# ScalarE copies ahead of the gate product, shorter score folds and fixed tree buffers in a two-layer transformer kernel

## The chip, the core and the metric

The kernel runs on one core of a Trainium2 chip. The metric is the device time of one execution in microseconds (us), as the median of several executions. A profile shows one further look at the kernel: one execution, recorded by the hardware profiler, whose times are counted from the first instruction ("the span"). The engines are called PE (TensorE, matrix products; PEld is its weight load), DVE (VectorE), ACT (ScalarE), POOL (GpSimd) and SP (SyncE, here the queue that issues nearly all DMAs).

## The reference

Two layers, each an attention block (A) and a gated feed-forward block (B), on x of 2048 tokens by 1024 features in bf16:

```python
x = x + A(layernorm(x), wqkv, wo)
x = x + B(layernorm(x), w1, w3, w2)      # twice, with the same weights

# A: 32 heads of 32; a token sees itself and 7 tokens before it, 2 apart
logits[h, s, w] = sum_d q[h, s, d] * k[h, s - 2*w, d] * scale     # w = 0..7
o[h, s, :] = sum_w softmax(logits)[h, s, w] * v[h, s - 2*w, :]
# B: F = 3584
out = (silu(x @ w1) * (x @ w3)) @ w2
```

So the attention has no large matrix product: each score is a sum over 32 products of a query and a shifted key, and each output a sum over 8 weighted values.

## The kernel before

**Units and stages.** The tokens are cut into chunks of 512 (`CH`), so each layer has four units (l, c). The feed-forward block of a unit is `b_stage`. After the first layer's q, k and v (`first_q`, `q_part`, to about 197 us in the profile), units 0 and 1 run plain products with w1, w3 and w2 and at the same time prepare the weights for what follows: sums of squares on ScalarE (`measure`, L854), a matmul with ones that adds them over the partitions (`scales`, L868, "size"), scaled copies on ScalarE (`copies`, L881), differences of blocks on VectorE (`differences`, L892) and stores of the blocks to DRAM on POOL's queue (L894, L895, tile `t_d`). This is called the preparing stage below (197 to 526 us). From unit 2 on (about 574 us to the end) `products` uses the stored blocks: each 2 by 2 block product is made of seven products P1 to P7 in place of eight (a Strassen scheme in Winograd's form).

**Product stage.** One group is 256 columns of hidden features of w1 (m = 0, the gate) or w3 (m = 1, the up product), two tiles of 128, over the four blocks of features and tokens. Each of the seven products is eight matmuls of 256 columns (`run`, L1102), into PSUM banks called A, B and D (tile `st`). `head_part` (L1120 to L1161) writes down the order: P1, P5, P6 and P2 of one group ("early") alternate with P7, P3 and P4 of the group before ("late"). Between them stand: ScalarE's copies of bank A to B after P1 (L1128), of D to the snapshot `s5` after P5 (L1133) and of A to `su` after P6 (L1137); VectorE's D += su (L1140), which P3 waits for, and s22 = A + s5 after P7 (L1150). Snapshots lie in the tile `big`. `consume` (L1106) takes the four results q = 0 (P2), 3 (P7), 1 (P3) and 2 (P4). For the gate group it is a Silu with a per-partition scale on ScalarE (L1111, tile `sg`), for the up group one `scalar_tensor_tensor` on VectorE (L1116): result times scale times gate, written as 16-bit floats into `hT` (`h16` is the same memory). The second product of the block, with w2, is `W` (L1028; matmuls L1037), fed by sums of `hT` blocks on VectorE (L1008).

**Attention.** It is done in halves of 256 tokens (`TCH`), sixteen in all, mostly on VectorE and beside TensorE's products of other units. `score_steps` multiplies q by a shifted k for each of eight offsets (L581: 128 partitions x 8 x 256, bf16) and folds the eight rows of each product to one by three additions (`tree`: 4 and 2 rows at L505, 1 row at L507) into `psm`. `gather_heads` (L594) adds the partitions of each head by four matmuls with 32 columns of weights, one to each quarter of the partitions of the PSUM tile `L`. The softmax follows on VectorE (L614, L617, L623, L625, L626) with the exponential on ScalarE (L618). `spread_heads` (L635) brings the weights back to all partitions by four matmuls, which ScalarE copies to `At` (L637). `value_steps` does the same with v (L665, the same `tree`) into `oT`, and `o_tile` (L770) multiplies by wo and adds to x (L775). The buffers of the products are the pool `scr`, four tiles of 4 KB a partition; a tree writes its folds in place.

**What sets the order.** The order of instructions on PE, DVE, ACT and SP is the order in which the Python code emits them, by hand. A small planner keeps clocks (`now`) with assumed costs. VectorE's background steps (norms, `makes` = the block differences, `adds`, values, scores) are generators, and `background(until)` (L136) places steps that end by that time ahead of the next foreground instruction. ScalarE's background (norm passes `act_norm`, L313 and L340; sums of squares of w2, L932) is placed by `act_background` (L356) when it ends within 2.2 us after TensorE's planned time. Gathers and spreads wait in `pe_queue` until 1.5 us past the planned end of their input (L559). `between` and `o_tile` place the wo products. The costs are constants in the code, such as 1.14 for a product, 0.605, 0.34 and 0.205 for the folds, and 0.69 for the up group's multiply. So an edit to a cost, or to the number of steps, moves all later background work on every queue.

Of the kernel before, what the change touches and what calls it, by code (L numbers as in the profile page):

```python
# [8 lines left out]
BF16 = mybir.dt.bfloat16  # L9
FP16 = mybir.dt.float16  # L10
I32 = mybir.dt.int32
ALU = mybir.AluOpType
# [5 lines left out]
def kernel(  # L18
# [52 lines left out]
    xtp = ctx.enter_context(tc.tile_pool(name="xnT", bufs=2))  # L71
    scr = ctx.enter_context(tc.tile_pool(name="scr", bufs=4))
    wk = ctx.enter_context(tc.tile_pool(name="wk", bufs=1))
# [23 lines left out]
    def dve(cost, ready=0.0):  # L97
        now["dve"] = max(now["dve"], ready) + cost
        return now["dve"]
# [85 lines left out]
    hT = const.tile([P, HTN, CH], BF16, name="hT")  # L185
    zero = wk.tile([P, W, TCH], BF16, name="psm")
    nc.vector.memset(zero[:, 0:2, :], 0.0)
# [11 lines left out]
    snaps = [big[:, 3072 + 1024 * i:4096 + 1024 * i].bitcast(FP32) for i in range(4)]  # L199
    snaps = [s_.rearrange("p (a t) -> p a t", a=2) for s_ in snaps]  # L200
    blocks = [big[:, 3584 * i:3584 * (i + 1)].rearrange("p (b k c) -> p b k c", b=7, k=KT // 2) for i in range(2)]
    NG = NF // FG
# [291 lines left out]

    def tree(n, mul, dst):

        bufs = {}

        def first(i):
            bufs[i] = mul(i)  # L500

        def half(i, m):
            b = bufs[i]
            if m > 1:
                nc.vector.tensor_tensor(b[:, 0:m, :], b[:, 0:m, :], b[:, m:2 * m, :], op=ALU.add)  # L505
            else:
                nc.vector.tensor_tensor(dst(i), b[:, 0, :], b[:, 1, :], op=ALU.add)  # L507

        def product(i):
            return 1.14, 0.0, lambda: first(i)  # L510

        def fold(i, m):
            return {4: 0.605, 2: 0.34, 1: 0.205}[m], 0.0, lambda: half(i, m)


        yield product(0)
        yield fold(0, 4)
        for i in range(0, n, 2):
            yield product(i + 1)
# [46 lines left out]
    def score_steps():  # L566

        V = nc.vector
        for g, (l, h) in enumerate(halves):
# [5 lines left out]
            qT, kT, ready = qks[l, h]  # L575
            psm = wk.tile([P, W, TCH], BF16, name="psm")

            def mul_qk(w_):
                pr = scr.tile([P, KT, TCH], BF16, name="pr", tag="scr")
                k0 = HALO - DIL * w_  # L580
                V.tensor_tensor(pr[:], qT[:], kT[:, :, k0:k0 + TCH], op=ALU.mult)  # L581
                return pr
# [8 lines left out]
            def gather_heads(t):  # L591
                at["L"] = L = side.tile([P, W, BLK], FP32, name="L", tag="sd")
                for a in range(4):
                    nc.tensor.matmul(L[32 * a:32 * (a + 1), :, :], lhsT=gather[:],  # L594
                                     rhs=psm[:, :, a * BLK:(a + 1) * BLK], start=True, stop=True)
                at["t"] = pe(3, t) + 0.2
# [49 lines left out]
    def value_steps():  # L646

        V = nc.vector
        for g, (l, h) in enumerate(halves):
# [10 lines left out]

            def mul_v(t):
                tm = scr.tile([P, W, TCH], BF16, name="tm", tag="scr")
                base = vT[:, t, HALO:HALO + TCH]
                win = bass.AP(vT.tensor, base.offset, [list(base.ap[0]), [-DIL, W], [1, TCH]])
                V.tensor_tensor(tm[:], At[:], win, op=ALU.mult)  # L665
                return tm
# [322 lines left out]
    def products(u, f0, f1, hold):  # L989
# [116 lines left out]
        def consume(G, q, src, r):  # L1106
            m, g, f = G["m"], G["g"], G["f"] + 2 * (q % 2)
            inv = down_scale[:, m, g:g + 1]
            if m == 0:
                sg = gates[g, q] = sgp.tile([P, 2, HT], BF16, name="sg", tag="sg")  # L1110
                nc.scalar.activation(sg[:], src, ACTF.Silu, scale=inv)  # L1111
                G["t", q] = act(0.6, r, "silu")
            else:
                background(r + 0.8)
                t0 = HT * (q // 2)
                nc.vector.scalar_tensor_tensor(h16[:, f:f + 2, t0:t0 + HT], src, inv, gates[g, q][:],  # L1116
                                               op0=ALU.mult, op1=ALU.mult)
                dve(0.69, r)

        def head_part(i, name):  # L1120
# [220 lines left out]
```

## Time and profile before

| | us |
|---|---|
| median of 4 executions | 1562.84 (1560.77 to 1565.59) |
| the profiled execution, own time | 1561.34 |
| its span, first to last instruction | 1559.6 |
| PE busy | 1536.5 |
| DVE busy | 1256.8 |
| ACT busy | 842.2 |
| POOL busy | 114.1 |
| granted PE clock, mean share | 0.997 |

By stage (us from the span's start):

| stage | length | PE busy | DVE busy | ACT busy |
|---|---|---|---|---|
| start, 0 to 31 | 31 | 28.68 | 17.05 | 14.15 |
| first q, k, v, 31 to 197 | 166 | 163.02 | 132.16 | 111.53 |
| preparing stage, 197 to 526 | 329 | 322.69 | 272.69 | 215.56 |
| q, k, v, 526 to 574 | 48 | 46.87 | 40.78 | 17.18 |
| product stage with later q, k, v, 574 to 1556 | 982 | 975.24 | 793.55 | 483.79 |

How such lines are read: a row of a group gives the source line, the engine, the operation, output and input tiles with their shapes, the number of instructions, then busy time in us and the mean in ns of one, then the idle time of the engine just before them and what ended it ("<-"). A row of the timeline gives start and length in us, and in brackets the idle time before with what ended it. A row of waits gives who waited for whom, the sum in us, how often, and the longest. Matmuls are pipelined: one of 512 columns is shown as 0.379 us long while the next starts after 0.216.

### The profile page before, as it was taken

The numbers are of one execution on the slowest core, as the hardware profiler recorded it, in microseconds if no ns is written. First come the engines' busy times: TensorE is split into PE (matmuls) and PEld (weight loads), VectorE is DVE, ScalarE is ACT, GpSimd is POOL, SyncE is SP. The second block draws the span as 40 slices with busy tenths as digits, with TensorE's granted clock in tenths as the row PEclk, the third lists the DMA queues.
The fourth block names the chain that finished last, engine by engine and source line by source line (L and its number), as shares of the span: only waits on it lengthen the run. The fifth ranks groups of instructions, "written<-read, shape, count | busy, mean of one in ns | idle before, by whom it ended". The sixth has DMA issues, their size and how long they took to land.

```text
span 1559.6 us, 24976 instructions
## 1 busy us (share of the span) xinstructions
PE 1536.5 (99%) x9666; PEld 995.6 (64%) x9666; DVE 1256.8 (81%) x2186; ACT 842.2 (54%) x1319; POOL 114.1 (7%) x227
## 2 busy tenths in 40 slices
PE   9999999999899999999999999999999999999999
PEld 7666544444444568575685766867667667686865
DVE  4788898978968889998989996999698997646545
ACT  4785567666738345546373555554647336353432
POOL 0110001111111000001000030000200001000000
PEclk9999999999999999999999999999999999999999
DMA  9766869797888888988789887797979887888885
GB/s 333 195 205 190 230 176 350 259 290 274 254 280 269 289 279 299 311 297 259 266 298 309 290 260 247 265 347 280 311 257 307 298 293 258 311 277 339 308 297 203
DMA packets 258359, 431.16 MB, mean 276 GB/s; under 512 B 72832, under 2 KB 200064, under 8 KB 241984
## 3 DMA queue, kind: packets, MB, share of 16 engines
q1 hardware_dynamic: 248464, 390.90, 75.9%
q0 software_dynamic: 9632, 38.54, 6.4%
q8 instruction: 75, 1.23, 0.3%
q14 instruction: 44, 0.36, 0.1%
q10 hardware_dynamic: 144, 0.13, 0.0%
HBM read 345.90 MB, written 67.90 MB: 265 GB/s over the span
## 4 chain that ended last, share of the span: by engine, by line
PE 60%; DVE 2%; DMA 2%; ACT 1%; POOL 1%; issue 1%; ACTq 0%; DVEq 0%
PE st L1102 32%; PE w L1037 15%; PE ps L828 8%; PE po L770 5%; DMA wqkv<-in_A_wqkv_dram 1%; DMA t_d<-big 1%; PE pe L635 1%; POOL acc L317 1%; DVE tm L665 0%; DMA xnT<-xn 0%; ACT big L965 0%; DVE hT L1008 0%; DVE tm L505 0%; ACT xn L313 0%; DVE big L288 0%
## 5 line engine op out<-in xcount | busy, mean ns | idle before, releaser
L828 PE MATMUL ps<-xnT,wqkv 128*128 128x512 f16 (+1 forms) x1472 | 323.2, 379 | 1.1 <-DMA wqkv<-in_A_wqkv_dram 1.1
L1102 PEld LDWEIGHTS <-early 128*128 128x128 f16 x2688 | 262.6, 98 | 40.7 <-issue 1.5
L828 PEld LDWEIGHTS <-wqkv 128*128 128x128 bf16 x1472 | 210.5, 144 | 109.5 <-issue 1.8
L1037 PE MATMUL w<-t,hT 128*128 128x512 f16 x1008 | 226.8, 379 | 1.1 <-ACT big L1057 1.0
L1102 PEld LDWEIGHTS <-late 128*128 128x128 f16 x2016 | 197.3, 98 | 30.2 <-issue 1.1
L581 DVE TENSOR_TENSOR pr<-qT,kT 128x2048 bf16<-128x2048 bf16 x128 | 155.9, 1218 | 26.7 <-DMA qT<-qkv_d 14.3
L1102 PE MATMUL st<-xnT,late 128*128 128x256 f16 x1344 | 174.2, 273 | 0.8 <-DVE big L1150 0.8
L1102 PE MATMUL st<-big,early 128*128 128x256 f16 x1344 | 172.7, 273 | 1.7 <-DVE big L288 1.2
L1037 PEld LDWEIGHTS <-hT 128*128 128x128 f16 x1008 | 98.1, 98 | 113.8 <-issue 2.7
L1102 PE MATMUL st<-xnT,early 128*128 128x256 f16 x1344 | 165.7, 273 | 0.0
L665 DVE TENSOR_TENSOR tm<-At,vT 128x2048 bf16<-128x2048 bf16 x128 | 155.9, 1218 | 10.7 <-ACT At L637 10.7
L505 DVE TENSOR_TENSOR pr<-pr 128x1024 bf16<-128x1024 bf16 (+1 forms) x256 | 137.8, 551 | 0.5
L505 DVE TENSOR_TENSOR tm<-tm 128x1024 bf16<-128x1024 bf16 (+1 forms) x256 | 137.2, 551 | 0.4
L770 PE MATMUL po<-wo,oT 128*128 128x512 bf16 x512 | 115.7, 379 | 0.4 <-DVE x_sb L775 0.4
L1128 ACT COPY st<-st 128x512 f32<-128x512 f32 x84 | 48.3, 575 | 124.2 <-PE st L1102 120.7
L1116 DVE SCALAR_TENSOR_TENSOR hT<-st,down_scale,sg 128x512 f16<-128x512 f32 x126 | 94.0, 746 | 20.5 <-PE st L1102 19.8
L1223 PE MATMUL pu<-xnT,w3t 128*128 128x512 f16 x448 | 107.5, 383 | 0.0
L1111 ACT ACTIVATE sg<-st,down_scale 128x512 bf16<-128x512 f32 x126 | 87.0, 691 | 36.1 <-PE st L1102 34.4
L1214 PE MATMUL pg<-xnT,w1t 128*128 128x512 f16 x448 | 106.4, 380 | 0.0
L1140 DVE TENSOR_TENSOR st<-st,big 128x512 f32<-128x512 f32 x84 | 58.5, 696 | 53.7 <-ACT big L1137 53.7
L832 ACT CAST hT<-ps 128x512 bf16<-128x512 f32 x96 | 55.2, 586 | 82.1 <-PE ps L828 81.1
L1243 PE MATMUL acc<-w2t,hT 128*128 128x512 bf16 x448 | 97.8, 379 | 0.0
(168 smaller groups left out, 1863.3 us busy)
## 6 DMA issues: line engine op xcount, KB each, us to landing
early<-t_d SPq DMA_DIRECT2D x84, 1024.0 KB, 5.8
late<-t_d SPq DMA_DIRECT2D x84, 768.0 KB, 6.3
t<-t_d SPq DMA_DIRECT2D x42, 1024.0 KB, 6.8
t<-t_d SPq DMA_DIRECT2D x42, 768.0 KB, 5.2
wqkv<-in_A_wqkv_dram SPq DMA_DIRECT2D x28, 1024.0 KB, 7.3
w1t<-in_B_w_dram SPq DMA_DIRECT2D x14, 1024.0 KB, 7.8
w3t<-in_B_w_dram SPq DMA_DIRECT2D x14, 1024.0 KB, 9.7
t_d<-big POOLq DMA_DIRECT2D x28, 512.0 KB, 6.1
```

What stands on the lines that cost most here:

```text
L505: nc.vector.tensor_tensor(b[:, 0:m, :], b[:, 0:m, :], b[:, m:2 * m, :], op=ALU.add)
L581: V.tensor_tensor(pr[:], qT[:], kT[:, :, k0:k0 + TCH], op=ALU.mult)
L665: V.tensor_tensor(tm[:], At[:], win, op=ALU.mult)
L770: nc.tensor.matmul(ps[:], lhsT=oT[:, t, j * P:(j + 1) * P], rhs=wo[:, t, hh * 512:(hh + 1) * 512], start=(t == 0), stop=(t == KT - 1))
L828: nc.tensor.matmul(ps[:], lhsT=ws[kk // KH][:, kk % KH, t::KT], rhs=xnT[:, kk, :], start=(kk == 0), stop=(kk == KT - 1))
L1037: nc.tensor.matmul(out[:], lhsT=lhs[:, k, j * P:(j + 1) * P], rhs=w[:, k, :], start=start and k == 0, stop=k == nq - 1, skip_group_check=True)
L1102: nc.tensor.matmul(out[:, a, :], lhsT=w[:, a, blk, k, :], rhs=rhs[:, k, :], start=start and a == 0 and k == 0, stop=k == KQ - 1, skip_grou ...
L1111: nc.scalar.activation(sg[:], src, ACTF.Silu, scale=inv)
L1116: nc.vector.scalar_tensor_tensor(h16[:, f:f + 2, t0:t0 + HT], src, inv, gates[g, q][:], op0=ALU.mult, op1=ALU.mult)
L1214: nc.tensor.matmul(pg[:], lhsT=w1t[:, kk, fi * P:(fi + 1) * P], rhs=xnT[:, kk, :], start=(kk == 0), stop=(kk == KT - 1))
L1223: nc.tensor.matmul(pu[:], lhsT=w3t[:, kk, fi * P:(fi + 1) * P], rhs=xnT[:, kk, :], start=(kk == 0), stop=(kk == KT - 1))
L1243: nc.tensor.matmul(acc[:], lhsT=hT[:, f, j * P:(j + 1) * P], rhs=tiles[hh][f // nq][:, f % nq, :], start=(f == 0), stop=(f == f1 - f0 - 1))
```

## The change

Three edits. First, in the up group, three of the four results (q = 0, 1, 2) are copied by ScalarE from PSUM to bf16 in SBUF, with the scale applied; the fourth (q = 3) gets its scale in s22 on VectorE, also as bf16. The multiply with the gate becomes a plain `tensor_tensor` of two SBUF tiles. Second, the score trees stop at two rows, `psm` is twice as large, and each half has eight gather matmuls, the second four adding to the first in PSUM. Third, the pool `scr` goes, and each of the two trees works in one fixed tile of 12 rows (6 KB a partition): even steps use rows 0 to 7 for the product, odd steps rows 4 to 11. The order of steps in the score tree changes with it. Planned costs change with the first edit (0.69 to 0.34 for the multiply, 0.5 for a copy).

```diff
-    scr = ctx.enter_context(tc.tile_pool(name="scr", bufs=4))
...
-    zero = wk.tile([P, W, TCH], BF16, name="psm")
+    tree_bufs = [const.tile([P, 12, TCH], BF16, name=f"tree{i}") for i in range(2)]
+    zero = tree_bufs[0]
...
+    tight = big[:, 6144:7168].bitcast(BF16).rearrange("p (i a t) -> p i a t", i=2, a=2)
...
-    def tree(n, mul, dst):
+    def tree(n, buf, mul, dst, partial):
         def first(i):
-            bufs[i] = mul(i)
+            mul(i, buf[:, 0:8, :] if i % 2 == 0 else buf[:, 4:12, :])
         def half(i, m):
-            b = bufs[i]
-            if m > 1:
-                nc.vector.tensor_tensor(b[:, 0:m, :], b[:, 0:m, :], b[:, m:2 * m, :], op=ALU.add)
+            b = buf[:, 0:4, :] if i % 2 == 0 else buf[:, 8:12, :]
+            if m == 4:
+                nc.vector.tensor_tensor(b, b, buf[:, 4:8, :], op=ALU.add)
+            elif m == 2 and not partial:
+                nc.vector.tensor_tensor(b[:, 0:2, :], b[:, 0:2, :], b[:, 2:4, :], op=ALU.add)
             else:
-                nc.vector.tensor_tensor(dst(i), b[:, 0, :], b[:, 1, :], op=ALU.add)
+                nc.vector.tensor_tensor(dst(i), b[:, 0:m, :], b[:, m:2 * m, :], op=ALU.add)
...
             yield product(i + 1)
             yield fold(i, 2)
             yield fold(i + 1, 4)
-            yield fold(i, 1)
+            if not partial:
+                yield fold(i, 1)
+            if partial and i + 2 < n:
+                yield product(i + 2)
             yield fold(i + 1, 2)
-            if i + 2 < n:
+            if not partial and i + 2 < n:
                 yield product(i + 2)
-            yield fold(i + 1, 1)
+            if not partial:
+                yield fold(i + 1, 1)
             if i + 2 < n:
                 yield fold(i + 2, 4)
...
-            psm = wk.tile([P, W, TCH], BF16, name="psm")
+            psm = wk.tile([P, W, 2, TCH], BF16, name="psm")
...
-            yield from tree(W, mul_qk, lambda w_: psm[:, w_, :])
+            yield from tree(W, tree_bufs[0], mul_qk, lambda w_: psm[:, w_], True)
...
-                for a in range(4):
-                    nc.tensor.matmul(L[32 * a:32 * (a + 1), :, :], lhsT=gather[:],
-                                     rhs=psm[:, :, a * BLK:(a + 1) * BLK], start=True, stop=True)
+                for i in range(2):
+                    for a in range(4):
+                        nc.tensor.matmul(L[32 * a:32 * (a + 1), :, :], lhsT=gather[:],
+                                         rhs=psm[:, :, i, a * BLK:(a + 1) * BLK], start=i == 0, stop=i == 1,
+                                         skip_group_check=True)
...
-            yield from tree(KT, mul_v, lambda t: oT[:, t, :])
+            yield from tree(KT, tree_bufs[1], mul_v, lambda t: oT[:, t, :], False)
...
-                background(r + 0.8)
+                if q != 3:
+                    up = tight[:, 1] if q == 2 else sgp.tile([P, 2, HT], BF16, name="up", tag="up", bufs=1)[:]
+                    nc.scalar.activation(up, src, ACTF.Copy, scale=inv)
+                    src, r = up, act(0.5, r)
+                background(r + 0.5)
                 t0 = HT * (q // 2)
-                nc.vector.scalar_tensor_tensor(h16[:, f:f + 2, t0:t0 + HT], src, inv, gates[g, q][:],
-                                               op0=ALU.mult, op1=ALU.mult)
-                dve(0.69, r)
+                nc.vector.tensor_tensor(h16[:, f:f + 2, t0:t0 + HT], src, gates[g, q][:], op=ALU.mult)
+                dve(0.34, r)
...
-                nc.scalar.copy(s5, G["D"][:])
+                nc.scalar.activation(s5, G["D"][:], ACTF.Copy, scale=down_scale[:, G["m"], G["g"]:G["g"] + 1] if G["m"] else 1.0)
...
-                nc.vector.tensor_tensor(s22, G["A"][:], s5, op=ALU.add)
+                if G["m"]:
+                    s22 = tight[:, 0]
+                    nc.vector.scalar_tensor_tensor(s22, G["A"][:], down_scale[:, 1, G["g"]:G["g"] + 1], s5,
+                                                   op0=ALU.mult, op1=ALU.add)
+                else:
+                    nc.vector.tensor_tensor(s22, G["A"][:], s5, op=ALU.add)
```

Beside this, `mul_qk` and `mul_v` write into the buffer that they are given.

More of the change, by code (lines that the diff above doesn't have):

```diff
@@ L493, in first_q @@
         qkv_at[0, 0, 0] = 28.0
-    def tree(n, mul, dst):
-        bufs = {}
+    def tree(n, buf, mul, dst, partial):
         def first(i):
-            bufs[i] = mul(i)
+            mul(i, buf[:, 0:8, :] if i % 2 == 0 else buf[:, 4:12, :])
         def half(i, m):
-            b = bufs[i]
-            if m > 1:
-                nc.vector.tensor_tensor(b[:, 0:m, :], b[:, 0:m, :], b[:, m:2 * m, :], op=ALU.add)
+            b = buf[:, 0:4, :] if i % 2 == 0 else buf[:, 8:12, :]
[3 more added lines that the diff above has]
+                nc.vector.tensor_tensor(b[:, 0:2, :], b[:, 0:2, :], b[:, 2:4, :], op=ALU.add)
             else:
-                nc.vector.tensor_tensor(dst(i), b[:, 0, :], b[:, 1, :], op=ALU.add)
+                nc.vector.tensor_tensor(dst(i), b[:, 0:m, :], b[:, m:2 * m, :], op=ALU.add)
         def product(i):
@@ L575, in score_steps, with mul_qk @@
             qT, kT, ready = qks[l, h]
-            psm = wk.tile([P, W, TCH], BF16, name="psm")
-            def mul_qk(w_):
-                pr = scr.tile([P, KT, TCH], BF16, name="pr", tag="scr")
+            psm = wk.tile([P, W, 2, TCH], BF16, name="psm")
+            def mul_qk(w_, pr):
                 k0 = HALO - DIL * w_
-                V.tensor_tensor(pr[:], qT[:], kT[:, :, k0:k0 + TCH], op=ALU.mult)
-                return pr
+                V.tensor_tensor(pr, qT[:], kT[:, :, k0:k0 + TCH], op=ALU.mult)
             yield 0.0, ready, lambda: None
-            yield from tree(W, mul_qk, lambda w_: psm[:, w_, :])
+            yield from tree(W, tree_bufs[0], mul_qk, lambda w_: psm[:, w_], True)
             load_v(l, h)
@@ L659, in value_steps, with mul_v @@
             oTs[l, h] = oT
-            def mul_v(t):
-                tm = scr.tile([P, W, TCH], BF16, name="tm", tag="scr")
+            def mul_v(t, tm):
                 base = vT[:, t, HALO:HALO + TCH]
                 win = bass.AP(vT.tensor, base.offset, [list(base.ap[0]), [-DIL, W], [1, TCH]])
-                V.tensor_tensor(tm[:], At[:], win, op=ALU.mult)
-                return tm
+                V.tensor_tensor(tm, At[:], win, op=ALU.mult)
             yield 0.0, max(ready, At_at[l, h]), lambda: None
-            yield from tree(KT, mul_v, lambda t: oT[:, t, :])
+            yield from tree(KT, tree_bufs[1], mul_v, lambda t: oT[:, t, :], False)
             oT_at[l, h] = now["dve"]
```

## The prediction

> **What bounds the kernel now.** I read first the page's busy times, then the waits of TensorE alone, then the timeline at the longest of these waits, and last the groups with shapes, for prices.
>
> ```profile
> PE 1536.5 (99%) x9666; PEld 995.6 (64%) x9666; DVE 1256.8 (81%) x2186; ACT 842.2 (54%) x1319; POOL 114.1 (7%) x227
> ```
>
> TensorE is the bound: 23 us of the 1559.6 us span are idle. A busy TensorE could still be slow, so I counted its work: about 4,570 matmuls of 512 columns at a start-to-start of 0.216 us (eight in 1.73 us in the timeline), 4,704 of 256 columns at 0.109 us, and some small ones, give about 1,520 us. What the change can win is therefore in this list, TensorE's waits (us in total, times, longest):
>
> ```profile
> PE size L868 <- ACT junk L854: 6.3, 3, 4.1
> PE pe L635 <- DVE E L626: 5.3, 2, 2.9
> PE pw L192 <- DVE psm L187: 1.2, 1, 1.2
> PE st L1102 <- DVE big L288: 1.2, 1, 1.2
> PE ps L828 <- DMA wqkv<-in_A_wqkv_dram: 1.1, 1, 1.1
> PE w L1037 <- ACT big L1057: 1.0, 2, 0.7
> ```
>
> Two spread matmuls (L635) wait 5.3 us for VectorE's softmax, and three size matmuls (L868) wait 6.3 us for ScalarE's sums of squares. The others behind VectorE or ScalarE are 1.2 + 1.0 here and 1.9 us below it (L1150 0.8, L1111 0.5, L775 0.4, L507 0.2). Counted from start to start each is 0.16 us longer, since a matmul's modelled end (0.379) runs past its place (0.216). This is the timeline of TensorE, then of VectorE, at one of the spreads:
>
> ```profile
> 934.96 0.40 PE L594 MATMUL L<-psm,gather 128*32 128x512 bf16 x4
> 935.29 10.58 PE L828 MATMUL ps<-xnT,wqkv 128*128 128x512 f16 x48
> 948.80 0.59 PE L635 MATMUL pe<-E,spread 128*128 128x512 bf16 x2 [2.93 <-DVE E L626]
> ```
>
> ```profile
> 941.79 0.69 DVE L288 TENSOR_TENSOR big<-xnT 128x1024 f16<-128x1024 f16 x1 [8.53 <-DMA xnT<-xn]
> 942.52 0.69 DVE L288 TENSOR_TENSOR big<-big,xnT 128x1024 f16<-128x1024 f16 x1
> 943.13 0.69 DVE L288 TENSOR_TENSOR xnT<-xnT 128x1024 f16<-128x1024 f16 x1
> ...
> 948.06 0.69 DVE L626 TENSOR_TENSOR E<-E,rs 128x512 bf16<-128x512 bf16 x1
> ```
>
> The softmax stood behind additions that waited for a transposed load: it is its place in the order, not VectorE's load, that made it late.
>
> **The prices**, from the groups with shapes (busy us, mean ns):
>
> ```profile
> L505 DVE TENSOR_TENSOR pr<-pr 128x512 bf16<-128x512 bf16 x128 | 53.5, 418 | 0.0
> L507 DVE TENSOR_TENSOR psm<-pr 128x256 bf16<-128x256 bf16 x128 | 36.5, 285 | 0.4
> L1116 DVE SCALAR_TENSOR_TENSOR hT<-st,down_scale,sg 128x512 f16<-128x512 f32 x126 | 94.0, 746 | 20.5 <-PE st L1102 19.8
> L1111 ACT ACTIVATE sg<-st,down_scale 128x512 bf16<-128x512 f32 x126 | 87.0, 691 | 36.1 <-PE st L1102 34.4 <-DVE st L1140 1.2
> L1218 ACT ACTIVATE sg<-pg 128x512 bf16<-128x512 f32 x56 | 32.5, 590 | 33.1 <-PE pg L1214 33.0
> L594 PE MATMUL L<-psm,gather 128*32 128x512 bf16 x64 | 6.4, 390 | 0.2 <-DVE psm L507 0.2
> ```
>
> VectorE instructions that do not depend on the one before start some 0.08 us before its end, so a place in its queue costs 0.20 us (256-wide fold), 0.33 (512-wide fold), 0.66 (gate multiply). One that depends starts 0.03 after it: the L288 pair above is 0.73 apart, the next 0.61, so **a dependence costs 0.12 us**.
>
> **The change, part by part.**
>
> *Gate multiply.* 168 multiplies of 0.66 us become plain products of 16-bit data in SBUF. The trace has no such product of bf16 with a 16-bit float result; its ends are 0.33 (L505, all operands 16 bit) and 0.66 (no gain, as rows with a PSUM operand). I take 0.33, the row with the same widths: 55 us of VectorE freed. ScalarE gets 126 scaled copies (the fourth product of an up group, after P7, reads a tile that VectorE itself has scaled) at 0.69 (L1111, pointer scale), 87 us, and 42 of its P5 copies get a pointer scale, 0.10 each by L1111 against L1218, 4 us: 842 becomes about 933 us. 42 additions L1150 take a scale, 0.69 to 0.75: 2.5 us. All this lies beside TensorE. What covers it: a product run is 0.87 us, a group seven, 6.1 us. ScalarE holds 4.5 us of this in a gate group (three copies, four Silus), in an up group 1.7 before and 3.9 after. P6 may start when the copy L1128 has read its bank, P7 after L1137; in the timeline near 1005 us these have 1.85 and 0.9 us to spare. ScalarE works in order, so a norm pass (L313, 1.06 + 0.19 us) ahead of the copies uses most of it; an up group then no longer catches up at once. Nothing in the trace shows how often that will pass the margin. From below: 0, since the one such wait now (L1111) is 0.5 us in 1,000. From above: see the third rival. I take **+2.0 us**, four times today's, as ScalarE's free time in a pair of groups falls from 6.0 to 3.8 us and three multiplies in four now wait on it. Behind such a multiply VectorE's other additions queue (L1140, for which P3 waits with 1.2 us or more to spare). The tile `up` has one buffer, so P3's copy waits for P2's product, and the bank copies wait behind it; but these stand four runs, 3.5 us, apart.
>
> The Trainium skill (ScalarE: Activation LUTs, Rules for kernel authors) speaks against this part: multiplications belong on VectorE. The rows agree that the exchange is poor in engine time, 0.69 given for 0.33 saved, 45 us in all; by that rule the change would lose, if engine time were what bounds.
>
> *Score folds.* 128 folds L507 of 0.20 us go: 26 us of VectorE, 1.6 a half. TensorE gets 64 more gathers. The four of one half start within 0.01 us of each other, as they use separate column groups, and the next matmul starts 0.32 us after the last. A second round on the same columns costs between 0.216 (matmuls of 512 columns following each other) and 0.322; with no overlap at all four would cost 0.86. I take 0.216: 16 x 0.216 = **+3.5 us**, all on the path.
>
> *Fixed buffers.* In the built order each product waits for the VectorE instruction right before it where it overwrites what that has just read: 7 of 8 products of a score tree, 4 of 8 of a value tree, 176 in all, at 0.12 us: up to 21 us of VectorE, less where foreground work comes between. The planner's costs do not hold it, so a gather may be planned 0.8 us too early; the gathers have 1.4 to 5 us of margin, but the first, which waits already: **+0.5 us**. The Trainium skill (VectorE: DVE Perf Modes, The DRAIN you can't avoid) has a semaphore between instructions cost nothing; by it these 21 and 0.5 us were nil. The 0.73 against 0.61 us above says otherwise.
>
> VectorE's net is 55 + 26 - 2.5 - 21, nearly 58 us, off the path.
>
> *What moves.* The planner puts background steps where VectorE is free, so the whole attention moves: in the built order gathers stand up to 90 us earlier in TensorE's sequence, with their q, k and v loads on the SP queue, equal in number and bytes. Then:
> - The spread at 180.54 us waited 2.6 us for an exponential behind a sum of squares whose load was late. Now the exponential stands ahead of those sums, and 14.7 us of matmuls lie between gather and spread (10.7 before): **-2.5**.
> - At 948.80 that half's softmax now is done some 60 us earlier: **-3.1** (start to start). Next late is the addition L288 for the product stage, ready at 944.4; TensorE comes there at about 949: no wait.
> - The other waits from 574 us on (L288, L1057, L1150, L1111, with the short ones 4.8 us by start-to-start) have VectorE or ScalarE queues as cause. Between none and all go; half: **-2.4**.
> - In the preparing stage (197 to 526 us) ScalarE is late. The size matmul at 384.50 waits 2.1 us, that at 482.50 0.35; the copies and exponential ahead of both have moved away: -2.4. But the next is this:
>
> ```profile
> 410.78 1.89 PE L1214 MATMUL pg<-xnT,w1t 128*128 128x512 f16 x8
> 416.82 0.58 PE L868 MATMUL size<-size,ones 128*128 128x1 f32 x2 [4.15 <-ACT junk L854]
> 417.26 3.57 PE L1223 MATMUL pu<-xnT,w3t 128*128 128x512 f16 x8
> ```
>
> Ahead of it an exponential with two table loads (1.28 each, 3.1 us in all) now stands, and the block differences whose stores the copies await come one to two steps later. Some of it falls into ScalarE's waits for stores (3.2 us). Between 0 and 6.4; I take 3.6. The eight matmuls after it take 3.57 instead of 1.89 us already. Together **+1.2**.
>
> **Sum**: 3.5 + 2.0 + 0.5 - 2.5 - 3.1 - 2.4 + 1.2 = -0.8 us. The profiled execution took 1561.34 us (span 1559.6 and 1.7 around it), so 1560.5; it lies 1.5 under the median of 1562.84, so **1562.0 us** as a median. About 0.3% (4.7 us) is what measurement can tell from no change.
>
> **Rivals.**
> *The cover holds everywhere.* ScalarE absorbs the copies, and every VectorE-side wait from 574 us on goes, as does the longer measure: 3.5 - 2.5 - 3.1 - 4.8 - 2.4 = -9.3 us, 1553.5. For it: in six stretches of product runs VectorE is busy 224.65 of 244 us and ScalarE 136.47, so the load goes to the freer engine. Against: the present order has eight such waits from 574 us on, and a new order will have some too.
> *The gate stays slow or the folds' gain never lands*: the products run at 0.66 because of their mixed types. Then VectorE gains nothing there, is level with today, and only -2.4 is lost: 1564.4, inside the forecast's own range.
> *ScalarE becomes late.* A pair of norm passes (2 x 1.25 us) exceeds the 2.2 us that an up group leaves by 0.3, and a spread copy (0.59) on top makes it 0.9. There are 32 such pairs in product runs (64 L313); if half meet a spread copy and push P6 or P7 back by that much, 16 x 0.9 = 14.4 us take the place of the 2.0: +11.6 us, **1574.4**. It decides once the lag passes P7's 0.9 us and P6's 1.85. Against: the planner counts the copies and holds norm passes back when ScalarE runs late.
> *The second gather round does not overlap*: 16 x 0.86 = 13.8 in place of 3.5, 1572.3. Against: separate columns, as now.
>
> **Chances**: forecast (with the slow-gate case) 0.46, cover holds 0.30, ScalarE late 0.17, gathers serial 0.07. The forecast's own range is 1558.2 to 1567. The range reaches into both sides: 1553 to 1571. Faster 0.30, same 0.46, slower 0.24.
>
> **What would show it.** Right: gate products near 0.42 us; eight gathers in about 0.54 us; no wait at L635 over 1 us; TensorE's idle near 20 us. Wrong: waits of product runs for L1128's or L1137's successors (ScalarE late); a wait near 415 us far over 8 us; gathers 0.2 us apart.

## The result, and the profile after

The changed kernel takes **1566.42 us** as a median of 31 executions (1561.69 to 1570.46), the kernel before 1562.43 in 51. The ratio is **1.0024, with a 95% interval of 1.0018 to 1.0030**: slower by 3.8 us, where the forecast was 0.8 us faster, and more than the interval leaves open. The profiled execution took 1564.80 us, with a span of 1563.1 (before 1561.34 and 1559.6). Lines of the changed kernel have moved: the gathers are L597, the spread L639, the sum over partitions L870, the products of the last stage L1104, the copies of up products L1118 and their multiply L1122.

The page's busy times of the changed kernel:

```profile
PE 1539.3 (98%) x9730; PEld 996.0 (64%) x9730; DVE 1193.1 (76%) x2058; ACT 928.1 (59%) x1445; POOL 109.9 (7%) x227
```

VectorE lost 63.7 us of work (58 forecast), ScalarE gained 85.9 (91 forecast), and TensorE has the 64 gathers more. VectorE's relief is as large as was counted, and the time is longer. TensorE's waits (us in total, times, longest):

```profile
PE size L870 <- ACT junk L856: 7.8, 1, 7.8
PE L L597 <- DVE psm L508: 2.1, 2, 1.6
PE po L772 <- DVE x_sb L777: 2.0, 2, 1.1
PE w L1039 <- ACT big L1059: 1.8, 3, 0.7
...
PE st L1104 <- ACT big L1142: 1.1, 2, 0.9
PE st L1104 <- ACT sg L1113: 1.1, 1, 1.1
```

The two spreads' waits, 5.3 us before, are gone altogether; those of the size matmuls, which led the list with 6.3 us, are one wait of 7.8. New or longer are the gathers (0.2 before), the wo products behind an addition (0.4 before), L1059 (1.0 before at L1057), and two behind ScalarE in the product stage. Counted from start to start (the waits over 0.1 us from 31 us on, without the usual step after a gather, and with what the matmuls of slow clock after the longest wait lose), they compare so, in us:

| stage | before | after | forecast of the change | measured |
|---|---|---|---|---|
| first q, k, v, to 197 us | 3.6 | 4.0 | -2.5 + 0.5 | +0.4 |
| preparing stage, to 527 | 9.4 | 10.6 | +1.2 | +1.2 |
| q, k, v, to 574 | 1.3 | 0 | 0 | -1.3 |
| product stage | 8.4 | 8.9 | -3.1 - 2.4 + 2.0 | +0.4 |
| second gather round | 0 | 3.5 | +3.5 | +3.5 |

The sum is +4.2; the span grew by 3.5, as the waits under 0.1 us came to 0.6 less and the end after the last matmul to 0.3 less, while the start, to 31 us, took 0.2 more. In this count the second round of gathers alone is as large as the loss. The waits, forecast to fall, came out nearly level: about as many new ones came as old ones went.

The groups behind the prices, with shapes (busy us, mean ns):

```profile
L1122 DVE TENSOR_TENSOR hT<-up,sg 128x512 f16<-128x512 bf16 x84 | 35.5, 423 | 47.0 <-ACT up L1118 46.4
L1118 ACT ACTIVATE up<-st,down_scale 128x512 bf16<-128x512 f32 x84 | 58.0, 690 | 13.8 <-PE st L1104 13.4
L508 DVE TENSOR_TENSOR psm<-tree 128x512 bf16<-128x512 bf16 x128 | 53.6, 419 | 0.4
L597 PE MATMUL L<-psm,gather 128*32 128x512 bf16 x128 | 9.8, 384 | 2.7 <-DVE psm L508 2.1 <-DVE x_sb L777 0.6
```

The multiply of two bf16 tiles into 16-bit floats takes 0.423 us, as the rows with the same widths said, and the copy 0.690. Eight gathers in TensorE's timeline:

```profile
873.74 0.61 PE L597 MATMUL L<-psm,gather 128*32 128x512 bf16 x8
874.29 1.05 PE L1104 MATMUL st<-big,early 128*128 128x256 f16 x8
```

The next matmul starts 0.55 us after the first gather (0.54 forecast). Within these eight the four of a round start within 0.01 us of each other, the second round 0.216 us after the last of the first, and the next matmul 0.312 us after the last gather: 16 x 0.22 = 3.5 us, as forecast.

### The profile page after: what moved, and what is told of

It is laid out like the page before. It is cut to its first block, busy times and chain, and to the rows that moved or that the text cites. A ratio compares the mean times of both kernels' runs of the same rounds, so it can differ in the third digit from the quotient of the medians.

```text
span 1563.1 us, 25163 instructions
## 1 busy us (share of the span) xinstructions
PE 1539.3 (98%) x9730; PEld 996.0 (64%) x9730; DVE 1193.1 (76%) x2058; ACT 928.1 (59%) x1445; POOL 109.9 (7%) x227
## 4 chain that ended last, share of the span: by engine, by line
PE 53%; DVE 9%; ACT 3%; DMA 2%; issue 1%; ACTq 0%; DVEq 0%; SPq 0%
PE st L1104 28%; PE w L1039 13%; PE ps L830 7%; PE po L772 4%; DVE tree L668 1%; DVE tree L584 1%; DVE tree L504 1%; DVE hT L1010 1%; DVE hT L1122 1%; DMA kT<-qkv_d 1%; DMA t_d<-big 0%; ACT sg L1113 0%; DVE x_sb L1024 0%; PE pe L639 0%; DMA xnT<-xn 0%
## 5 line engine op out<-in xcount | busy, mean ns | idle before, releaser
L1104 PEld LDWEIGHTS <-early 128*128 128x128 f16 x2688 | 262.7, 98 | 41.4 <-issue 2.8
L1104 PEld LDWEIGHTS <-late 128*128 128x128 f16 x2016 | 197.0, 98 | 32.9 <-issue 3.3
L584 DVE TENSOR_TENSOR tree<-qT,kT 128x2048 bf16<-128x2048 bf16 x128 | 156.2, 1221 | 35.3 <-DMA kT<-qkv_d 18.5
L504 DVE TENSOR_TENSOR tree<-tree 128x1024 bf16<-128x1024 bf16 x256 | 175.1, 685 | 0.8
L1104 PE MATMUL st<-xnT,late 128*128 128x256 f16 x1344 | 174.2, 273 | 1.3 <-ACT big L1142 1.1
L1104 PE MATMUL st<-big,early 128*128 128x256 f16 x1344 | 172.4, 273 | 1.2 <-ACT sg L1113 1.1
L1104 PE MATMUL st<-xnT,early 128*128 128x256 f16 x1344 | 166.0, 273 | 0.0
L668 DVE TENSOR_TENSOR tree<-At,vT 128x2048 bf16<-128x2048 bf16 x128 | 156.1, 1220 | 11.2 <-ACT At L641 10.0
L1133 ACT COPY st<-st 128x512 f32<-128x512 f32 x84 | 48.4, 577 | 111.5 <-PE st L1104 110.7
L1113 ACT ACTIVATE sg<-st,down_scale 128x512 bf16<-128x512 f32 x126 | 86.6, 687 | 12.4 <-PE st L1104 12.1
L772 PEld LDWEIGHTS <-oT 128*128 128x128 bf16 x512 | 50.0, 98 | 59.3 <-issue 3.8
L1104 PE MATMUL st<-big,late 128*128 128x256 f16 x672 | 87.1, 273 | 0.0
```

Source lines behind the costliest of these rows:

```text
L504: nc.vector.tensor_tensor(b, b, buf[:, 4:8, :], op=ALU.add)
L584: V.tensor_tensor(pr, qT[:], kT[:, :, k0:k0 + TCH], op=ALU.mult)
L668: V.tensor_tensor(tm, At[:], win, op=ALU.mult)
L772: nc.tensor.matmul(ps[:], lhsT=oT[:, t, j * P:(j + 1) * P], rhs=wo[:, t, hh * 512:(hh + 1) * 512], start=(t == 0), stop=(t == KT - 1))
L1104: nc.tensor.matmul(out[:, a, :], lhsT=w[:, a, blk, k, :], rhs=rhs[:, k, :], start=start and a == 0 and k == 0, stop=k == KQ - 1, skip_grou ...
```

## Experiments

All times are medians; the kernel before ran beside them on the same chip (1562.2 in the first four, 1563.14 in the next four, 1562.73 in the last four). The three groups ran on three chips, so runs are compared by their ratios.

| kernel | us | ratio to before | 95% interval |
|---|---|---|---|
| gathers issued twice | 1564.81 | 1.0017 | 1.0006 to 1.0027 |
| changed, full folds | 1562.42 | 1.0002 | 0.9993 to 1.0010 |
| before, up copies only | 1569.50 | 1.0046 | 1.0033 to 1.0058 |
| changed, roots on GpSimd | 1564.68 | 1.0013 | 1.0004 to 1.0021 |
| before, fixed 6 KB buffers only | 1559.60 | 0.9979 | 0.9968 to 0.9989 |
| changed, no up copies | 1563.89 | 1.0007 | 0.9996 to 1.0017 |
| changed, differences first | 1562.30 | 0.9992 | 0.9982 to 1.0001 |
| before, gathers planned later | 1574.68 | 1.0076 | 1.0062 to 1.0091 |
| before, fixed buffers that do not overlap | 1563.31 | 1.0003 | 0.9993 to 1.0013 |
| gathers planned later, fixed 6 KB buffers | 1569.31 | 1.0042 | 1.0028 to 1.0056 |
| fixed 6 KB buffers, differences first | 1564.12 | 1.0010 | 1.0000 to 1.0020 |
| changed, planner's costs mended | 1570.98 | 1.0056 | 1.0040 to 1.0071 |

The theory at the start was: the second gather round is the loss, and the other two edits cancel. The rivals were that the copies on ScalarE are the loss, and that VectorE's relief wins something which the folds take back.

### The gathers alone

```diff
-                for a in range(4):
+                for i in range(2):
+                    for a in range(4):
```

The kernel before, each of its gather rounds issued twice (the second writes the same values again).

> The kernel before with each round of four gather matmuls (L594) issued twice, the second writing the same scores again; nothing else and no order is changed. Theory (the change's loss is its 64 extra gathers, all on TensorE's path): +3.5 us, 16 x 0.216, ratio 1.0022, with TensorE's other waits as before. Rival (the gathers slip into gaps, the loss is ScalarE's or the trees'): ratio 1.000. If the second round ran one by one: +13.8 us, 1.009.

1.0017, which is 2.7 us: 3.5 lies inside the interval, free gathers and gathers that do not overlap outside it. The list of waits stayed much as before (6.3 us for the size matmuls, 4.9 for the spreads). The round costs what its place costs.

### The changed kernel without the short folds

```diff
-            psm = wk.tile([P, W, 2, TCH], BF16, name="psm")
+            psm = wk.tile([P, W, TCH], BF16, name="psm")
-            yield from tree(W, tree_bufs[0], mul_qk, lambda w_: psm[:, w_], True)
+            yield from tree(W, tree_bufs[0], mul_qk, lambda w_: psm[:, w_, :], False)
```

and four gathers as before.

> The changed kernel with the score trees folded to one row again and four gathers a half; up copies and fixed buffers stay. Theory: VectorE gets back 128 folds of 0.20 us (26 us) and nobody waits for it, so the 3.5 us of gathers come off: ratio to before 1.000, between 0.999 and 1.0015. Rival (ScalarE's copies or the fixed buffers cost the time): it stays at 1.0024.

1.0002: with full folds the rest of the change comes to nothing. Taken from the changed kernel's 1.0024 the folds with their gathers cost 0.0022, 3.4 us. That the other two edits each come to nothing does not follow, and the next runs show that they do not.

### The up copies alone, and a GpSimd instruction of 7.78 us

The kernel before with L1118's copies, the scale at P5 and the s22 with a scale, the tree buffers and folds as they were.

> The kernel before with the up copies on ScalarE alone (first edit), old trees and four gathers. Theory: 55 us of VectorE freed and 90 us of ScalarE added, both beside TensorE; ratio 1.000 within 0.0015 either way, with ScalarE-side waits (L1137, L1111) of some 2 us in place of VectorE-side ones. Rival (ScalarE late is the loss): 1.002 or more. Rival (the cover holds): 0.996.

1.0046, 7.2 us slower, far more than expected. In its TensorE timeline most of it stands in one place:

```profile
768.60 0.62 PE L595 MATMUL L<-psm,gather 128*32 128x512 bf16 x4 [6.61 <-DVE psm L508]
```

The score folds stood behind additions that waited for a transposed load, the load waited for a norm pass on ScalarE, and the norm pass for GpSimd, whose timeline holds a very long instruction, on 128x4 numbers:

```profile
739.97 7.78 POOL L318 TENSOR_SCALAR acc<-acc 128x4 f32<-128x4 f32 x1 [16.02 <-ACT xn L314]
```

The same instruction takes 0.23 us as a median of its 20 in this run. What holds it for 7.78 us is told below, where two more runs show it.

### The roots of the background norms on GpSimd

The wait of 7.8 us has ahead of it, on ScalarE, an exponential with two table loads, and the norms' square roots load tables as well.

```diff
-                nc.scalar.activation(sd[:], mv[:, :, 1], ACTF.Sqrt, bias=epst[:])
+                nc.gpsimd.tensor_scalar(sd[:], mv[:, :, 1], 0.0, EPS, op0=ALU.max, op1=ALU.add)
+                nc.gpsimd.tensor_tensor(sd[:], sd[:], powers[:], op=ALU.pow)
...
```

GpSimd computes the inverse root, so VectorE's reciprocal after it goes too.

> The changed kernel with the square root of the background norms (L237 before) moved from ScalarE to two small POOL instructions, so that the four table loads (5.1 us) ahead of the longest wait of TensorE are gone. Theory (that wait, 7.8 us at 427.87, is ScalarE's queue): it falls to about 2.7 us, the eight slow matmuls behind it (1.6 us) go, and the time falls by 5 to 8 us, ratio to before 0.997 to 0.999. Rival (the stores that the copies wait for bind it): the wait falls by 1 to 2 us only, ratio 1.0015.

The wait stayed at 7.8 us, and the whole won 1.7 us against the changed kernel (1.0013 against 1.0024). Fewer table loads do not shorten it, so the rival stands: something that ScalarE's copies wait for. Here are the wait in TensorE's timeline and, in ScalarE's, a copy that waited for the store of an earlier block, `t_d` (changed kernel):

```profile
427.87 0.58 PE L870 MATMUL size<-size,ones 128*128 128x1 f32 x2 [7.84 <-ACT junk L856]
428.31 3.51 PE L1233 MATMUL pu<-xnT,w3t 128*128 128x512 f16 x8
```

```profile
416.75 0.72 ACT L883 ACTIVATE big<-w3t,up_scale 128x512 f16<-128x512 bf16 x1 [2.69 <-DMA t_d<-big]
```

That store is issued behind differences on VectorE (L894), and these stood behind norm steps in VectorE's order.

### The differences first

```diff
-            for queue in (norms, makes, adds, values, scores):
+            for queue in (makes, norms, adds, values, scores):
```

> The changed kernel, where background work on VectorE takes the differences of weight blocks ahead of norm steps when both could start at once (one tuple of queues in another order). The 7.8 us wait of TensorE at 427.87 us for the size matmuls goes back, by the rival that the last run left standing, to a DMA that lands late, whose store was issued behind differences that stood behind norm steps on VectorE. If so, the store comes 2 to 3 us earlier, the wait falls to 4 to 6 us, and with less slow clock after it the time falls by 2 to 5 us: 1561.5 to 1564.5, ratio near 1.0005. If the copies themselves bind, the wait stays at 7 to 8 us and the time at 1566.

The wait fell as the theory has it, a little further than the 4 to 6 us expected (changed kernel with this edit):

```profile
PE size L870 <- ACT junk L856: 3.8, 1, 3.8
```

4.0 us less, and 0.9992 in place of 1.0024, 5 us. ScalarE's copies there no longer wait for the store (2.69 us in the changed kernel). So about half of the 7.8 us was bound by a norm step ahead of a difference in VectorE's queue, two engines and a store away from TensorE; the 3.8 that are left are about what the kernel before had (4.1).

### The kernel before in another order

```diff
-        while pe_queue and limit and (must or pe_queue[0][0]() + 1.5 <= now["pe"]):
+        while pe_queue and limit and (must or pe_queue[0][0]() + 2.0 <= now["pe"]):
```

The kernel before, with no work added or removed: gathers, spreads and wo products go into TensorE's queue a little later.

> The kernel before with the same work in another order: gathers, spreads and output products are let into TensorE's queue when they are planned to be ready 2.0 us earlier, in place of 1.5. Nothing is added or removed. Theory (chance waits: each new order of the background work brings about as many waits as it removes, in other places, and the sum of a new order can't be read from the list of waits of the old one): the 4.9 us for the spread go or shrink, as they do in the changed kernel, yet the time moves by less than the waits removed, to between 1558 and 1567, with new waits in TensorE's list. Rival (waits removed are time won, as the prediction counted them): the spread's waits of 4.9 us go and the time falls by 2.5 to 5 us, to 1557.5 to 1560.

1574.68, 12 us slower: both expectations were too low, the sign of the rival's was wrong. Of the spreads' two waits one stayed (2.3 us). The longest waits now are 7.3 us for a size matmul and this one in TensorE's timeline:

```profile
933.28 3.15 PE L828 MATMUL ps<-xnT,wqkv 128*128 128x512 f16 x7 [5.70 <-ACT hT L832]
```

ScalarE could not copy the products out, because a norm pass ahead of the copies waited for GpSimd. Here are ScalarE's line and then GpSimd's:

```profile
931.52 1.24 ACT L340 ACTIVATE xn<-x_sb,mom 128x1024 f16<-128x1024 bf16 x1 [13.68 <-POOL mom L323]
```

```profile
916.49 15.00 POOL L323 TENSOR_SCALAR mom<-mom 128x2 f32<-128x2 f32 x1
```

15.00 us for 128x2 numbers; the median of this line is 0.235. All through it VectorE ran value trees, each instruction starting 0.08 us before the one ahead had ended, for 27 instructions, up to here:

```profile
930.96 0.42 DVE L505 TENSOR_TENSOR tm<-tm 128x512 bf16<-128x512 bf16 x1
931.42 0.29 DVE L507 TENSOR_TENSOR oT<-tm 128x256 bf16<-128x256 bf16 x1
```

The last fold needs the result of the one right before it and so starts 0.03 us after its end. It is the first break in VectorE's run, and GpSimd's instruction ends at 931.48. The kernel before has the same at the place that the prediction dwelt on. Its GpSimd timeline:

```profile
924.69 8.33 POOL L317 TENSOR_SCALAR acc<-acc 128x4 f32<-128x4 f32 x1 [17.73 <-ACT xn L313]
```

It ends at 933.02; VectorE's first break after 924.69 is at 932.98. The norm pass on ScalarE then starts at 935.34, the transposed load reaches VectorE's additions at 941.79 (the 8.53 us in the prediction's timeline), and the spread waits until 948.80.

The Trainium skill (SBUF — State Buffer, Who interferes with whom) says that a VectorE instruction with two inputs in SBUF contends with a GpSimd instruction that reads SBUF, and that the one which comes second is blocked until the other's end. The rows agree on who blocks whom; but here the block outlasts one instruction, up to 27 of them.

### Fixed buffers alone

The kernel before with the two fixed tree tiles, full folds, four gathers, the multiply as it was. The order of instructions on TensorE and SyncE is that of the kernel before.

> The kernel before with the fixed 6 KB tree buffers alone: full folds, four gathers, no copies of up products. Its products now wait for the fold whose operand they overwrite, which gave +34 ns against -83 ns, 0.117 us for each held product on VectorE, and nothing is added on TensorE. Theory (the loss is the second gather round, the rest comes to nothing): 1562.4, ratio 1.000 within 0.001, TensorE busy as before. Rival (the fixed buffers alone cost time, and the up copies give it back): above 1563.8, ratio over 1.001, with more idle time of TensorE at the gathers' wait for the folded products.

Both expectations fell: it is **faster than both kernels, 0.9979** (0.9968 to 0.9989). The spread's wait of 2.9 us at 948.80 is gone, and in GpSimd's timeline the long instruction too:

```profile
925.89 0.74 POOL L318 TENSOR_SCALAR acc<-acc 128x4 f32<-128x4 f32 x1 [17.72 <-ACT xn L314]
926.71 0.70 POOL L319 TENSOR_TENSOR mom<-acc 128x2 f32<-128x2 f32 x1
```

VectorE has 6.5 us more busy time, and 71 of its 256 tree products start 0.03 us after the fold before them. Within a tree these are every second product, so such a break comes every eight instructions, 4.7 us. A new theory: the breaks let GpSimd in. VectorE's timeline beside the two instructions:

```profile
925.33 1.22 DVE L584 TENSOR_TENSOR tree<-qT,kT 128x2048 bf16<-128x2048 bf16 x1
926.47 0.28 DVE L508 TENSOR_TENSOR psm<-tree 128x256 bf16<-128x256 bf16 x1
...
927.39 1.23 DVE L584 TENSOR_TENSOR tree<-qT,kT 128x2048 bf16<-128x2048 bf16 x1
```

They bear the theory out only in part. L319 ended at 927.41, at the break before the product of 927.39; but L318 ended at 926.63, 0.08 us after a product, where VectorE's next fold was already running and left no break.

### Fixed buffers without the breaks

```diff
-    tree_bufs = [const.tile([P, 12, TCH], BF16, name=f"tree{i}") for i in range(2)]
+    tree_bufs = [const.tile([P, 16, TCH], BF16, name=f"tree{i}") for i in range(2)]
...
-            mul(i, buf[:, 0:8, :] if i % 2 == 0 else buf[:, 4:12, :])
+            mul(i, buf[:, 0:8, :] if i % 2 == 0 else buf[:, 8:16, :])
...
```

The fold of four rows follows the new place of the odd products.

> The kernel before with fixed tree buffers of 8 KB, in which even and odd trees do not overlap, so that no product waits for the fold right before it; otherwise as the run with fixed 6 KB buffers, which has the same order as the kernel before and was faster, 0.9979. Theory: the fixed 6 KB buffers won because each held product leaves a break of some 0.03 us in VectorE's queue, in which a GpSimd instruction gets in; in the kernel before one of 128x4 elements (usual 0.22 us) took 8.33 us from 924.69 us, until VectorE's first break, and the norm pass, the transposed load and the spread at 948.80 us were late behind it. Without the breaks a GpSimd instruction of over 5 us and the wait of some 3 us near 948 us come back, and the time goes to 1562, ratio 0.999 to 1.001. Rival (the fixed addresses as such win): 1559.6, ratio 0.998, no such wait.

1.0003: the win is gone, the wait is back (2.9 us at 950.88), and so is this in GpSimd's timeline:

```profile
926.78 8.32 POOL L318 TENSOR_SCALAR acc<-acc 128x4 f32<-128x4 f32 x1 [17.73 <-ACT xn L314]
```

What wins in the fixed buffers is that they overlap. Whether at this place the breaks themselves spared GpSimd, or that its instruction now met VectorE's run at another point, these two runs do not tell apart.

### The bad order with the breaks

The kernel with gathers planned 2.0 us later, with the fixed 6 KB buffers.

> The kernel before in the other order (planned 2.0 us before, 1.0076) with the fixed 6 KB tree buffers added. In that order a GpSimd instruction on the norm's moments took 15.00 us from 916.49 us, behind VectorE's unbroken run of value trees, and TensorE stood 5.7 us at 933.28 us behind ScalarE, whose norm pass waited for it. Theory (GpSimd locked out of SBUF, let in at the breaks of held products): no GpSimd instruction over 4 us, the 5.7 us go, and the time falls by 5 to 12 us, to 1563 to 1570, ratio 1.000 to 1.005. Rival (it is the order alone): 1573 to 1576, ratio over 1.006.

1.0042 in place of 1.0076, 5.3 us; the 5.7 us wait is gone, and the 15.00 us have become this:

```profile
916.73 3.29 POOL L324 TENSOR_SCALAR mom<-mom 128x2 f32<-128x2 f32 x1
```

It ends at 920.02, at VectorE's first break after its start, a held product at 919.96. So here a break does end the hold, in a second order and at a second place. Over all profiles the same shows: each of the five kernels without overlapping buffers has one GpSimd instruction of 7.8 to 15.0 us, and none of the nine with them has one over 3.30. The other 6.6 us of that order stay: a size matmul (7.0), two late loads (2.4 each), and others.

### The changed kernel without the up copies

The gate multiply reads PSUM again; short folds, eight gathers and fixed buffers stay.

> The changed kernel without the copies of the up products: score folds that stop at two partials, eight gathers and fixed buffers only, the gate multiply from PSUM as before. Theory (the loss is the second gather round, 16 x 0.21 = 3.4 us, and the copies come to nothing): 1566, ratio 1.0022, between 1.0014 and 1.0030. Rival (the copies cost and the folds are free): 1562.4, ratio 1.000. Rival (the copies win about 2 us by relieving VectorE, as was forecast): above 1567.5, ratio over 1.0033.

1.0007, between the theory's 1.0022 and the 1.000 of the rival that the folds are free. With the run of fixed buffers the change can now be put together one edit after another: fixed buffers 0.9979, then short folds and gathers 1.0007, then up copies 1.0024. That is **-3.3, +4.4 and +2.7 us**, together +3.8. In the other order the copies cost 1.0002 - 0.9979, 3.6 us, and the folds 3.4. Each step is the difference of two ratios and by their intervals good to about 2 us.

### A version to beat both

Fixed 6 KB buffers with the differences first.

> Meant to beat both kernels: fixed 6 KB buffers alone (0.9979) with differences of weight blocks taken ahead of norm steps, which took 4 us off the changed kernel. Here the size matmuls' waits are 1.2 us at 387 and 4.1 us at 419 us. If the same cause holds, they fall by 1 to 3 us, and the time goes to 1557 to 1559, ratio 0.996 to 0.9975. Rival (a new order brings its own waits): 1559.6 or more.

1.0010, slower than fixed buffers alone. The wait at 419 us fell from 4.0 to 1.3 us, as meant, but the one at 388 rose from 1.1 to 2.2, and loads that had not been waited for, or less, came in: 2.5 us for a block of w2 at 427 and 2.7 (0.9) for wqkv at 543. The rival was right: what cured one order is no cure in another.

### The planner's costs mended

```diff
-            return 1.14, 0.0, lambda: first(i)
+            held = i > 0 and (partial or i % 2 == 1)
+            return 1.14 + 0.12 * held, 0.0, lambda: first(i)
...
-                    src, r = up, act(0.5, r)
+                    src, r = up, act(0.6, r)
```

> The changed kernel with the planner's costs mended: a held product 1.26 us in place of 1.14, the copy of an up product 0.6 in place of 0.5. Theory (gathers were planned too early by the dependences): the gathers' waits for the folded products at 61.93 and 577.64 us, 2.5 us by start to start, fall under 1 us, and the time goes to 1564 to 1565.5, ratio 1.001 to 1.002. Rival (the new order brings as much elsewhere): 1566 or more, ratio over 1.0022.

1.0056, 5 us slower than the changed kernel. The gathers' waits fell from 1.6 to 1.0 us at the first and vanished at 577, though one at 156 us grew from 0.6 to 1.1, and the 7.8 us became 3.6; but a spread waits 3.5 us again, and two more size matmuls 2.1. Truer costs gave a worse order. Which of its waits make up the 5 us was not followed up.

## Why the prediction was wrong, point by point

1. *Gathers, +3.5*: **right**. 0.216 us from round to round, 0.55 us for eight, 3.5 us in the profile; issued twice in the kernel before, 2.7 (0.9 to 4.2).
2. *Gate multiply at 0.33 a place, copies at 0.69*: **right** (0.423 and 0.690 long), as were VectorE's relief (63.7 against 58) and ScalarE's load (928 against 933).
3. *ScalarE late, +2.0*: **the size right by luck, the mechanism wrong**. Waits of product runs behind ScalarE (L1133, L1142, L1113) are 3.2 us by start to start against 1.1 before, and the copies as a whole cost 2.7 to 3.6 us in the runs. But the two of over 1 us stand behind the exponential with its two table loads, not behind a pair of norm passes. ScalarE's timeline in the changed kernel, and TensorE's wait for it:

```profile
875.98 1.28 ACT L622 ACT_TABLE_LOAD   x1
877.27 0.60 ACT L622 ACTIVATE E<-L 128x512 bf16<-128x512 f32 x1
877.88 1.28 ACT L1113 ACT_TABLE_LOAD   x1
879.18 0.69 ACT L1113 ACTIVATE sg<-st,down_scale 128x512 bf16<-128x512 f32 x1
```

```profile
879.92 1.03 PE L1104 MATMUL st<-big,early 128*128 128x256 f16 x8 [1.09 <-ACT sg L1113]
```

   3.2 us of exponential, against P7's 0.9 and P6's 1.85 us to spare.
4. *Dependence of 0.12 us, gathers planned too early, +0.5*: the dependence is **right** (0.03 after the end against 0.08 before it). Only 89 of the 176 products start after such a break (the prediction took 176 as the most). The size on TensorE was off: 1.7 us at the first gather (0.4 before) and 0.7 at 577.64, +2.0. And the sign of the edit as a whole was wrong: alone it wins 3.3 us.
5. *The spread at 180.54, -2.5*: it went, but that stage has other waits in its place, 1.7 and 0.8 for gathers and 1.3 for a wo product: 3.6 us became 4.0.
6. *The spread at 948.80, -3.1*: it went, and the reason was incomplete. "The softmax stood behind additions that waited for a transposed load": the load was late because GpSimd had been held 8.33 us by VectorE's trees. With the order unchanged, the overlapping buffers remove the wait, and buffers that do not overlap bring it back. So this gain can come from the edit that the prediction booked as a loss; in the changed kernel, where the gather also stands 61 us earlier (873.74 against 934.96), the two reasons are not told apart.
7. *Half of the other waits from 574 us on, -2.4*: **failed**. L288's went and L1150's shrank from 0.8 to 0.2 us, but L1057's grew from 1.0 to 1.8, and others came (879.92, 1176.52, 1254.82 us, each 1.0 to 1.3): the stage's 8.4 us became 8.9 even with the spread's 3.1 gone.
8. *Preparing stage, +1.2*: **right** (+1.2): the waits at 384.50 and 482.50 went, the long one grew from 4.3 to 8.0 (3.6 forecast). It was put down to the exponential and to stores; taking the differences first, which frees the stores, took 4.0 us off it with the exponential still ahead.

**The step that failed** is the booking of removed waits as won time: -2.5, -3.1 and -2.4 against +2.0 and +0.5 for what the new order brings. Most of the waits that were to go went, and as much came in other places: the first stage, -2.0 by forecast, came out at +0.4, and the product stage, -3.5 without the gathers, at +0.4. That is no accident of this change. One constant of the planner, with no work added, moved the time by 12 us; truer costs moved it by 5 the wrong way; the differences first won 5 us in one order and lost 5 in another. A list of waits belongs to one order. What held best are the terms that do not depend on the order: the price of a place on TensorE and the durations. Of the prediction's signs of being right, the gate product (0.423), the eight gathers (0.55) and no wait at a spread all came, and only the idle time (23.8 us, about 20 forecast) spoke against it.

What stays open: what a break has to do with it, as GpSimd's small instructions mostly get in between VectorE's within about 1 us even without one (at 45.62 us in the kernel before, 1.06 us), and now and then not for 8 or 15; where the other half of the 7.8 us comes from; and which waits make the copies' 2.7 to 3.6 us in full, which was read from the lists and not tried one by one. Whether fixed buffers with full folds can be bettered was tried once, without success.

## What to carry to other kernels

When TensorE is 98% busy and a planner places the rest, price what a change puts on TensorE, and do not book relief of an engine beside it as won time: here the waits were shuffled more than removed, and one perturbation without work in it (here a constant, 12 us) tells how far. When a wait ends at a chain, follow it to its root, through the small engines too: one tiny instruction of 8 us on GpSimd was the cause of a 3 us wait two engines later. Measure each edit of a change apart: here one of three won 3.3 us, and the other two lost 7.

## What the runs showed of the hardware

- A GpSimd instruction on 128x2 or 128x4 numbers (0.22 us) can be held for 8.3 or 15.0 us by an unbroken run of VectorE additions and products of SBUF tiles. In the cases of 7.8 us and more it ended within 0.1 us of VectorE's first break, 0.03 us wide, which an instruction makes that needs the one before it. Where VectorE began an addition with an operand in PSUM, one of 3.07 us ended as well (at 1313.92 us in the kernel before). Overlapping buffers, which make such breaks at 6.5 us of VectorE's time, left none over 3.30 us and won 3.3 us; that breaks end a hold is shown for such of 3.3 us, not for the place of the win.
- After TensorE had waited 7.84 us, eight matmuls took 3.51 us in place of 1.89, with a granted clock of 0.91 in the stretch from 400 to 440 us; after 4.15 us, in the kernel before, it was much the same. Part of a long wait's price comes after it.
